# Decode attention beside a gated MLP: two-head tiles, product sums as identity matmuls, p.v with the values moving, a row maximum, one load queue

## The chip, the cores and the metric

The kernel runs on one core of one Trainium2 chip. The metric is the device time of a launch in microseconds, as the median of several runs; it was 710.52 us before the change (three runs, 710.52 to 710.72). A core has five engines with instruction queues of their own: TensorE (PE, matmuls; its weight loads are listed as PEld), VectorE (DVE), ScalarE (ACT), GpSimd (POOL) and SyncE (SP). Loads are issued from an engine's queue and moved by 16 DMA engines.

## What is computed

One decode step for four sequences: a layernorm of the input x, then attention over a cache of 4096 keys and values per head (32 heads of 128, each with its own keys and values), and beside it a small gated MLP on the same normalised input; both are added to x. Data are bf16.

```python
xn = layernorm(x)                                  # x: 4 x 1 x 640
q = (xn @ wq).reshape(4, 1, 32, 128).transpose(0, 2, 1, 3)
scores = einsum('bhqd,bhkd->bhqk', q, k_cache) * 128 ** -0.5   # k_cache: 4 x 32 x 4096 x 128
p = softmax(scores, axis=-1)
o = einsum('bhqk,bhkd->bhqd', p, v_cache)
A = o.transpose(0, 2, 1, 3).reshape(4, 1, 4096) @ wo           # wo: 4096 x 640

z = gelu(einsum('bsd,df->bsf', xn, w_in))          # w_in: 640 x 1728
z1, z2 = z[..., :864], layernorm(z[..., 864:])
g = einsum('ts,bsf->btf', w_sp, z2) + b_sp
B = einsum('bsf,fd->bsd', z1 * g, w_out)           # w_out: 864 x 640
return x + A + B
```

Keys and values are 2 x 134 MB; the weights together are some 14 MB. There is one query per head, so every key and value is used once.

## The kernel before

The main loop (L375) runs over 128 pairs of a head and a sequence, `idx = 4 * h + b`. For each, K and V of that head (4096 x 128, 1 MB each) lie in SBUF with 32 consecutive positions to each of the 128 lanes, so each lane holds one run of 8 KB. `issue_kv` (L113) loads them four iterations ahead, K from SP's queue (L118) and V from ScalarE's (L123), into pools of six buffers each.

Within an iteration:

- TensorE spreads the query row over all lanes by a matmul with a column of the identity (L391), and ScalarE copies it to bf16 (`qbc_sb`, L399).
- VectorE multiplies K by it (L402, 128 x 4096 elements), then sums the 128 products of each position: three halving additions from 128 to 16 elements (L411, 2048, 1024 and 512 elements a lane), and one reduction of the last 16 (L418). The scores are a 128 x 32 tile.
- ScalarE takes the exponential with the scale in it, and its sum over the lane goes into a column of `acc` (L425). No maximum is subtracted.
- TensorE forms p.v with V as the stationary operand: 32 matmuls, each of which loads 128 x 128 values and moves one column of p (L458). The result is a column of 128 values, copied to `o_all` by ScalarE (L466).

After four iterations (one head of all four sequences, L470) the lane sums are added by a matmul with ones (L473), inverted on VectorE (L481), spread over the lanes (L483), multiplied into the columns (L486), and the head's part of the output projection is added into a PSUM tile by two matmuls (L495, L502).

The queries are made in eight chunks of 512 columns (`compute_q_chunk`, five matmuls each, L196), and the pieces of wq and wo are loaded as the loop goes. The gated MLP is spread over iterations 16 to 28: its first projection (L217), the gelu, the layernorm, and its output projection (L348). At the end x, the MLP's part and the attention's part are added and stored (L516 to L519).

The order of instructions on each engine is found by the framework's scheduler. Engines are in-order queues: an instruction that waits holds up all that stands behind it on its engine.

Of the kernel before, what the change touches and what calls it, by code (L numbers as in the profile page):

```python
# [13 lines left out]
ALU = mybir.AluOpType  # L14

KV_BUFS = int(os.environ.get("PSGQA_KV_BUFS", "4"))
KV_SLACK = int(os.environ.get("PSGQA_KV_SLACK", "2"))
V_ENG = os.environ.get("PSGQA_V_ENG", "scalar")
RED_W = int(os.environ.get("PSGQA_RED_W", "16"))
O_COPY_ENG = os.environ.get("PSGQA_OCOPY", "scalar")  # L20
GMLP_AT = int(os.environ.get("PSGQA_GMLP_AT", "16"))
S_BUFS = int(os.environ.get("PSGQA_S_BUFS", "4"))
T_BUFS = int(os.environ.get("PSGQA_T_BUFS", "2"))
PV_ROW = int(os.environ.get("PSGQA_PV_ROW", "0"))
# [3 lines left out]
def kernel(  # L28
# [16 lines left out]

# [6 lines left out]
    NH = Bsz * H  # L52
    FHC = 108
    assert Fh % FHC == 0
    NFC = Fh // FHC
    NBLK = S // P
    scale_qk = float(Dh) ** -0.5
    eps = 1e-5
    assert Dh == P and HD == H * Dh
    N0 = 512  # L60
    NQC = HD // N0
    HPQ = N0 // Dh
    ITER_PER_CHUNK = HPQ * Bsz
    NZC = 2 * NFC
    NHALF = D // 2

    const = ctx.enter_context(tc.tile_pool(name="const", bufs=1))
    wts = ctx.enter_context(tc.tile_pool(name="wts", bufs=1))
    work = ctx.enter_context(tc.tile_pool(name="work", bufs=2))
    kpool = ctx.enter_context(tc.tile_pool(name="kpool", bufs=KV_BUFS + KV_SLACK))  # L70
    vpool = ctx.enter_context(tc.tile_pool(name="vpool", bufs=KV_BUFS + KV_SLACK))
    spool = ctx.enter_context(tc.tile_pool(name="spool", bufs=S_BUFS))
    tpool = ctx.enter_context(tc.tile_pool(name="tpool", bufs=T_BUFS))
    gpool = ctx.enter_context(tc.tile_pool(name="gpool", bufs=3))
    wqp = ctx.enter_context(tc.tile_pool(name="wqp", bufs=3))
    wop = ctx.enter_context(tc.tile_pool(name="wop", bufs=3))
    ps_misc = ctx.enter_context(tc.tile_pool(name="ps_misc", bufs=2, space=bass.MemoryType.PSUM))
    ps_out = ctx.enter_context(tc.tile_pool(name="ps_out", bufs=1, space=bass.MemoryType.PSUM))
    ps_q = ctx.enter_context(tc.tile_pool(name="ps_q", bufs=2, space=bass.MemoryType.PSUM))
    ps_o = ctx.enter_context(tc.tile_pool(name="ps_o", bufs=2, space=bass.MemoryType.PSUM))  # L80

    wsp_bf = const.tile([1, 1], BF16)
    nc.sync.dma_start(out=wsp_bf[:], in_=B_w_sp[0:1, 0:1])
    bsp_bf = const.tile([1, 1], BF16)
    nc.sync.dma_start(out=bsp_bf[:], in_=B_b_sp.rearrange("(a b) -> a b", a=1))
    x_bf = const.tile([Bsz, D], BF16)
    nc.sync.dma_start(out=x_bf[:], in_=A_x.flatten_outer_dims())

    wq_v = A_wq.rearrange("(c p) n -> p c n", p=P)
    wq_tiles = {}  # L90

    def issue_wq(j):
        if j < 0 or j >= NQC or j in wq_tiles:
            return
        wq_sb = wqp.tile([P, DC, N0], BF16)
        nc.sync.dma_start(out=wq_sb[:], in_=wq_v[:, :, j * N0 : (j + 1) * N0])
        wq_tiles[j] = wq_sb

    wo_v = A_wo.rearrange("(j hh p) n -> j p hh n", hh=HPQ, p=P)
    wo_tiles = {}  # L100

    def issue_wo(j):
        if j < 0 or j >= NQC or j in wo_tiles:
            return
        wo_sb = wop.tile([P, HPQ, D], BF16)
        nc.sync.dma_start(out=wo_sb[:], in_=wo_v[j])  # L106
        wo_tiles[j] = wo_sb

    issue_wq(0)

    kv_tiles = {}

    def issue_kv(i):  # L113
        if i >= NH or i in kv_tiles:
            return
        hh, bb = divmod(i, Bsz)
        k_nat = kpool.tile([P, NBLK, Dh], BF16)
        nc.sync.dma_start(  # L118
            out=k_nat[:], in_=A_k_cache[bb, hh].rearrange("(p c) d -> p c d", c=NBLK)
        )  # L120
        v_nat = vpool.tile([P, NBLK, Dh], BF16)
        veng = {"gpsimd": nc.gpsimd, "sync": nc.sync, "scalar": nc.scalar}[V_ENG]
        veng.dma_start(  # L123
            out=v_nat[:], in_=A_v_cache[bb, hh].rearrange("(p c) d -> p c d", c=NBLK)
        )
        kv_tiles[i] = (k_nat, v_nat)

    for i in range(KV_BUFS):
        issue_kv(i)
    issue_wo(0)  # L130
    issue_wq(1)
    issue_wo(1)

    w_in_sb = wts.tile([P, DC, F], BF16)
    nc.sync.dma_start(out=w_in_sb[:], in_=B_w_in.rearrange("(c p) n -> p c n", p=P))
    w_out_sb = wts.tile([FHC, NFC, D], BF16)
    nc.sync.dma_start(  # L137
        out=w_out_sb[:], in_=B_w_out.rearrange("(c p) n -> p c n", p=FHC)
    )

    ident = const.tile([P, P], BF16)
    make_identity(nc, ident[:])
    ones_col = const.tile([P, 1], FP32)
# [4 lines left out]
    nc.vector.memset(eps_tile[:], eps)  # L148

# [5 lines left out]
    for i in range(NSTAT):  # L155
# [5 lines left out]
        out=rstd[:],  # L161
        in_=mv[:, 1:2],
        func=ACT.Sqrt,
        bias=eps_tile[:Bsz],
        scale=1.0,
# [11 lines left out]
    xnT_ps = ps_misc.tile([P, DC, Bsz], BF16, tag="m")  # L177
    for c in range(DC):
        nc.tensor.transpose(
            out=xnT_ps[:, c, :],  # L180
            in_=xn_bf[:, c * P : (c + 1) * P],
            identity=ident[:Bsz, :Bsz],
        )
    xnT_sb = const.tile([P, DC, Bsz], BF16)
    nc.vector.tensor_copy(out=xnT_sb[:], in_=xnT_ps[:])

    q_rows = const.tile([Bsz, HD], BF16)
    q_done = set()

    def compute_q_chunk(j):  # L190
        if j in q_done or j >= NQC:
            return
        wq_sb = wq_tiles.pop(j)
        q_ps = ps_misc.tile([Bsz, N0], FP32, tag="m")
        for c in range(DC):
            nc.tensor.matmul(  # L196
                out=q_ps[:],
                lhsT=xnT_sb[:, c, :],
                rhs=wq_sb[:, c, :],
                start=(c == 0),  # L200
                stop=(c == DC - 1),
            )
        nc.vector.tensor_copy(out=q_rows[:, j * N0 : (j + 1) * N0], in_=q_ps[:])  # L203
        q_done.add(j)

    compute_q_chunk(0)

    res_sb = const.tile([Bsz, D], FP32)
    gm = {}

    def gmlp_stage_zT(k0, k1):
        if "zT_ps" not in gm:
            gm["zT_ps"] = ps_misc.tile([FHC, NZC, Bsz], FP32, tag="m", name="zT_ps")
        zT_ps = gm["zT_ps"]
        for k in range(k0, k1):
            for c in range(DC):
                nc.tensor.matmul(  # L217
                    out=zT_ps[:, k, :],
                    lhsT=w_in_sb[:, c, k * FHC : (k + 1) * FHC],
                    rhs=xnT_sb[:, c, :],  # L220
                    start=(c == 0),
                    stop=(c == DC - 1),
                )

    def gmlp_stage_gelu():
        zT_ps = gm["zT_ps"]
        zz = work.tile([FHC, NZC, Bsz], FP32)
        nc.vector.tensor_copy(out=zz[:], in_=zT_ps[:])
        gw = work.tile([FHC, NZC, Bsz], FP32)
        nc.vector.tensor_tensor(out=gw[:], in0=zz[:], in1=zz[:], op=ALU.mult)  # L230
        nc.vector.tensor_scalar(
            out=gw[:],
            in0=gw[:],
            scalar1=0.044715,
            scalar2=1.0,
            op0=ALU.mult,
            op1=ALU.add,
        )
        nc.vector.tensor_tensor(out=gw[:], in0=gw[:], in1=zz[:], op=ALU.mult)
        gt = work.tile([FHC, NZC, Bsz], FP32)  # L240
# [6 lines left out]
        gz = work.tile([FHC, NZC, Bsz], FP32)  # L247
        nc.vector.tensor_tensor(out=gz[:], in0=zz[:], in1=gt[:], op=ALU.mult)
        gm["gz"] = gz
        sq = work.tile([FHC, NFC, Bsz], FP32)  # L250
# [3 lines left out]
        gm["sq"] = sq  # L254

    def gmlp_stage_ln():
        gz = gm["gz"]
        sq = gm["sq"]
        wsp_t = work.tile([1, 1], FP32)
        nc.vector.tensor_copy(out=wsp_t[:], in_=wsp_bf[:])  # L260
        bsp_t = work.tile([1, 1], FP32)
        nc.vector.tensor_copy(out=bsp_t[:], in_=bsp_bf[:])
        s_ps = ps_misc.tile([1, 2 * Bsz], FP32, tag="m")
        for k in range(NFC):
            nc.tensor.matmul(
                out=s_ps[:, 0:Bsz],
                lhsT=ones_col[:FHC, :],
                rhs=gz[:, NFC + k, :],
                start=(k == 0),
                stop=(k == NFC - 1),  # L270
            )
        for k in range(NFC):
            nc.tensor.matmul(
                out=s_ps[:, Bsz : 2 * Bsz],
                lhsT=ones_col[:FHC, :],
                rhs=sq[:, k, :],
                start=(k == 0),
                stop=(k == NFC - 1),
            )
        st = work.tile([1, 5 * Bsz], FP32)  # L280
# [5 lines left out]
        inv_fh = 1.0 / float(Fh)  # L286
        nc.vector.tensor_scalar(
            out=mean_t, in0=s_ps[:, 0:Bsz], scalar1=inv_fh, scalar2=None, op0=ALU.mult
        )
        nc.vector.tensor_scalar(  # L290
            out=ex2_t,
            in0=s_ps[:, Bsz : 2 * Bsz],
            scalar1=inv_fh,
# [6 lines left out]
            out=rst_t, in_=var_t, func=ACT.Sqrt, bias=eps_tile[:1], scale=1.0  # L300
        )
        nc.vector.reciprocal(out=rst_t, in_=rst_t)
        ACrow = work.tile([1, 2 * Bsz], FP32)
        nc.vector.tensor_scalar(
            out=ACrow[:, 0:Bsz],
            in0=rst_t,
# [68 lines left out]
    for idx in range(NH):  # L375
# [11 lines left out]
        for fn in gmlp_schedule.get(idx, []):  # L387
            fn()
# [161 lines left out]
```

## Time and profile before

| | |
|---|---|
| median of three runs | 710.52 us |
| profiled execution, from first to last instruction | 707.1 us |
| read from HBM in it | 282.24 MB |
| VectorE busy | 644.0 us |
| TensorE matmuls busy | 230.7 us |
| ScalarE busy | 94.8 us |
| loads, 100 to 660 us | 418 GB/s |
| loads, 683 to 707 us | 25 GB/s |
| product L402, 128 x 4096 | 2282 ns |
| halving additions L411, 2048 / 1024 / 512 elements | 1215 / 681 / 413 ns |
| reduction L418, 512 elements to 32 | 671 ns |
| exponential L425 and its sum | 229 + 187 ns |
| matmul L495, 512 columns | 586 ns |
| f32 matmul L483, 128-column weights: weight load / matmul | 306 / 360 ns |

A page of a profile is the record of one execution. "Busy" is the time in which an engine carried out instructions. In a line of the groups, the name of the tile written stands left of the arrow and those read stand right of it; then come the shapes, the number of instructions, the busy time in us, the mean ns of one, and the idle time just before them with what ended it. An f32 matmul appears as two instructions. The 40 slices show shares of busy time in tenths along the span, and PEclk the clock that was granted to TensorE, in tenths of full speed.

### The profile page before, as it was taken

What the parts mean: (1) busy time and instruction counts of PE and PEld (TensorE: products, weight loads), DVE (VectorE), ACT (ScalarE), POOL (GpSimd) and SP (SyncE); (2) the same over time, 40 slices, a digit from 0 to 9 for tenths busy, and PEclk for the clock granted to TensorE, in tenths of its full rate; (3) what the DMA queues carried; (4) which work ended last, traced back from release to release, by engine and by line L of the source; (5) the groups of instructions that cost most, each with busy time, mean ns of one, the idle gap of its engine ahead of it and who ended that gap; (6) DMA issues with size and microseconds to landing.
All of it is one profiled execution on the core that took longest, in us unless ns stands there. A gap on an engine that the chain in (4) does not pass through costs nothing.

```text
span 707.1 us, 11278 instructions
## 1 busy us (share of the span) xinstructions
PE 230.7 (33%) x4591; PEld 171.6 (24%) x4591; DVE 644.0 (91%) x747; ACT 94.8 (13%) x519; POOL 0.7 (0%) x6
## 2 busy tenths in 40 slices
PE   1211243635343243322333342223433234332332
PEld 0110122523222222222222222222222222222221
DVE  1925999999999999999999989999999999999996
ACT  0200111111211111111011111111111111111110
POOL 0000000000000000000000000000000000000000
PEclk9999999999975555555555555555555555555555
DMA  8999999999999999999999999999999999999960
GB/s 348 403 359 411 419 419 406 417 416 420 412 421 419 416 420 412 419 417 419 419 413 421 416 420 421 420 413 416 421 420 421 420 419 421 419 421 420 419 273 1
DMA packets 47940, 282.99 MB, mean 400 GB/s; under 512 B 4392, under 2 KB 14480, under 8 KB 15120
## 3 DMA queue, kind: packets, MB, share of 16 engines
q1 hardware_dynamic: 29456, 148.04, 51.6%
q10 hardware_dynamic: 18432, 134.23, 45.9%
q8 instruction: 36, 0.59, 0.3%
q14 instruction: 16, 0.13, 0.0%
HBM read 282.24 MB, written 0.01 MB: 399 GB/s over the span
## 4 chain that ended last, share of the span: by engine, by line
DVE 64%; DMA 22%; PE 6%; issue 4%; SPq 3%; ACT 0%; DVEq 0%; ACTq 0%
DVE tmp L402 31%; DVE tmp L411 28%; DMA k_nat<-in_A_k_cache_dram 21%; DVE s_sb L418 3%; PE bc_ps L483 2%; PE q_ps L196 2%; SPq L118 2%; SPq L106 1%; DMA v_nat<-in_A_v_cache_dram 1%; PE g_ps L348 1%; DVE q_rows L203 1%; SPq L137 1%; PE out_ps L495 1%; DVE recip L481 0%; DVE o_norm L486 0%
## 5 line engine op out<-in xcount | busy, mean ns | idle before, releaser
L402 DVE TENSOR_TENSOR tmp<-k_nat,qbc_sb 128x4096 bf16<-128x4096 bf16 x128 | 292.0, 2282 | 24.0 <-DMA k_nat<-in_A_k_cache_dram 22.7
L411 DVE TENSOR_TENSOR tmp<-tmp 128x2048 bf16<-128x2048 bf16 (+2 forms) x384 | 282.4, 770 | 0.1
L458 PEld LDWEIGHTS <-v_nat 128*128 128x128 bf16 x4096 | 124.6, 104 | 423.3 <-issue 364.6
L458 PE MATMUL o_ps<-p_sb,v_nat 128*128 128x1 bf16 x4096 | 127.0, 165 | 225.9 <-ACT p_sb L425 203.9
L391 PE MATMUL qbc_ps<-q_rows,ident 4*128 4x128 bf16 x128 | 34.1, 269 | 170.9 <-ACT qbc_sb L399 170.2
L418 DVE TENSOR_REDUCE s_sb<-tmp 128x32 f32<-128x512 bf16 x128 | 85.7, 671 | 0.0
L425 ACT ACTIVATE p_sb<-s_sb 128x32 bf16<-128x32 f32 x128 | 29.4, 229 | 258.1 <-DVE s_sb L418 235.2
L399 ACT CAST qbc_sb<-qbc_ps 128x128 bf16<-128x128 f32 x128 | 32.8, 258 | 176.7 <-DVE tmp L402 107.7
L466 ACT COPY o_all<-o_ps 128x1 f32<-128x1 f32 x128 | 20.3, 159 | 165.0 <-PE o_ps L458 157.1
L483 PE MATMUL bc_ps<-recip,ones_row 1*128 1x4 f32 x64 | 18.7, 360 | 51.6 <-DVE recip L481 51.6
L483 PEld LDWEIGHTS bc_ps<-recip,ones_row 1*128 1x128 f32 x64 | 15.9, 307 | 55.2 <-DVE recip L481 55.2
L425 ACT ACTIVATION_READ_ACCUMULATOR p_sb<-s_sb 128x1 f32 x128 | 23.9, 187 | 0.2
L196 PE MATMUL q_ps<-wq_sb,xnT_sb 128*4 128x512 bf16 x40 | 19.8, 624 | 6.4 <-DMA wq_sb<-in_A_wq_dram 6.4
L495 PE MATMUL out_ps<-wo_sb,o_norm 128*4 128x512 bf16 x32 | 19.1, 598 | 8.4 <-DVE o_norm L486 8.4
L203 DVE CAST q_rows<-q_ps 4x512 bf16<-4x512 f32 x8 | 5.4, 678 | 16.9 <-PE q_ps L196 16.9
L486 DVE TENSOR_TENSOR o_norm<-o_all,bc_ps 128x4 bf16<-128x4 f32 x32 | 5.1, 158 | 8.0 <-PE bc_ps L483 7.9
L391 PEld LDWEIGHTS <-ident 4*128 4x128 bf16 x128 | 9.4, 105 | 8.3 <-issue 7.1
L502 PE MATMUL out_ps<-wo_sb,o_norm 128*4 128x128 bf16 x32 | 10.0, 312 | 0.0
L217 PE MATMUL zT_ps<-xnT_sb,w_in_sb 128*108 128x4 bf16 x80 | 7.8, 233 | 0.0
L217 PEld LDWEIGHTS <-w_in_sb 128*108 128x108 bf16 x80 | 7.6, 216 | 0.6 <-issue 0.5
L196 PEld LDWEIGHTS <-xnT_sb 128*4 128x4 bf16 x40 | 3.9, 110 | 13.7 <-issue 13.2
L481 DVE RECIPROCAL recip<-den_ps 1x4 f32<-1x4 f32 x32 | 5.3, 164 | 2.0 <-PE den_ps L473 2.0
(59 smaller groups left out, 40.5 us busy)
## 6 DMA issues: line engine op xcount, KB each, us to landing
v_nat<-in_A_v_cache_dram ACTq DMA_DIRECT2D x128, 1024.0 KB, 12.0
k_nat<-in_A_k_cache_dram SPq DMA_DIRECT2D x128, 1024.0 KB, 19.8
wq_sb<-in_A_wq_dram SPq DMA_DIRECT2D x8, 640.0 KB, 20.0
wo_sb<-in_A_wo_dram SPq DMA_DIRECT2D x8, 640.0 KB, 18.7
w_in_sb<-in_B_w_in_dram SPq DMA_DIRECT2D x1, 2160.0 KB
w_out_sb<-in_B_w_out_dram SPq DMA_DIRECT2D x1, 1080.0 KB
wsp_bf<-in_B_w_sp_dram SPq DMA_DIRECT2D x1, 0.0 KB
bsp_bf<-in_B_b_sp_dram SPq DMA_DIRECT2D x1, 0.0 KB
```

The costliest lines, as they stand in the source:

```text
L196: nc.tensor.matmul(out=q_ps[:], lhsT=xnT_sb[:, c, :], rhs=wq_sb[:, c, :], start=(c == 0), stop=(c == DC - 1),)
L217: nc.tensor.matmul(out=zT_ps[:, k, :], lhsT=w_in_sb[:, c, k * FHC : (k + 1) * FHC], rhs=xnT_sb[:, c, :], start=(c == 0), stop=(c == DC - 1),)
L391: nc.tensor.matmul(out=qbc_ps[:], lhsT=ident[:Bsz, b : b + 1].to_broadcast([Bsz, P]), rhs=q_rows[:, h * Dh : (h + 1) * Dh], start=True, st ...
L399: nc.scalar.copy(out=qbc_sb[:], in_=qbc_ps[:])
L402: nc.vector.tensor_tensor(out=tmp[:], in0=k_nat[:], in1=qbc_sb[:, None, :].to_broadcast([P, NBLK, Dh]), op=ALU.mult,)
L411: nc.vector.tensor_tensor(out=tmp[:, :, 0:h2], in0=tmp[:, :, 0:h2], in1=tmp[:, :, h2:w], op=ALU.add,)
L418: nc.vector.tensor_reduce(out=s_sb[:], in_=tmp[:, :, 0:w], axis=mybir.AxisListType.X, op=ALU.add,)
L425: nc.scalar.activation(out=p_sb[:], in_=s_sb[:], func=ACT.Exp, scale=scale_qk, accum_out=acc[:, col : col + 1],)
L458: nc.tensor.matmul(out=o_ps[:, :], lhsT=v_nat[:, c, :], rhs=p_sb[:, c : c + 1], start=(c == 0), stop=(c == NBLK - 1),)
L466: nc.scalar.copy(out=o_all[:, col : col + 1], in_=o_ps[:])
L483: nc.tensor.matmul(out=bc_ps[:], lhsT=ones_row[:, :], rhs=recip[:], start=True, stop=True)
L495: nc.tensor.matmul(out=out_ps[:, 0:N0], lhsT=lhsT, rhs=cur_wo[:, hh, 0:N0], start=first_proj, stop=last,)
```

## The change

The attention is written anew; the gated MLP's arithmetic stays.

- **Tiles.** A tile is now two heads of one sequence. The 2 x 4096 positions are laid over the lanes with 64 consecutive ones each, so lanes 0 to 63 hold the first head and 64 to 127 the second, and each lane has one run of 16 KB. There are 64 such tiles. K and V share one pool of seven 16 KB slots, and all loads are issued from SP's queue, K before V; at the end both last K tiles come before the last two V tiles, and the last V in four parts. All of wq is loaded first, into the same slots. The weights are laid out so that a lane's run is contiguous.
- **Queries.** All eight chunks are made before the loop, and copied by ScalarE.
- **Scores.** The products are formed on VectorE as before, in two halves of 32 positions. Their sums from 128 to 16 are made on TensorE: eight matmuls with the identity as weights, which add eight groups of 16 columns into one PSUM bank. VectorE reduces the last 16.
- **Maximum.** For each tile VectorE takes the maximum over a lane, TensorE turns the column of 128 into a row, VectorE takes the (negated) maximum of each half, and two f32 matmuls spread it, scaled, back over the lanes as the bias of the exponential.
- **p.v.** p is kept in a zeroed tile of 8 columns per position, one column for each of the two heads and four sequences. A matmul takes 4 positions (32 columns) as weights and moves 512 columns of V; 16 of them make a tile. They add into a 32 x 512 PSUM tile over four sequences, in which only blocks on the diagonal are wanted.
- **Groups.** After four tiles (two heads of all sequences) `group_a` to `group_d` copy that tile, add the lane sums, pick and add the diagonal blocks with f32 matmuls, normalise, turn, and project. They are spread over two iterations.
- **Sums at the end.** x and the MLP's part are added into the output's PSUM tile by matmuls.
- **Order.** On TensorE, VectorE and ScalarE the loop's order is the order in which it is written.

```diff
+KV_SLOTS = 7
+KV_AHEAD = 6
...
+    for c0, c1 in ((0, 2), (2, 4), (4, 5)):
+        t = kv.tile([P, 2, HD], BF16, tag="kv", name="wq")
+        nc.sync.dma_start(out=t[:, 0 : c1 - c0, :], in_=wq_v[:, c0:c1, :])
...
+    def load_k(i):
+        if i < NT:
+            k_tiles[i] = kv.tile([P, NC, Dh], BF16, tag="kv", name="k_nat")
+            nc.sync.dma_start(out=k_tiles[i][:], in_=kv_view(A_k_cache, i))
...
+    load_to(4)
+    nc.sync.dma_start(out=w_in_sb[:], in_=B_w_in.rearrange("(p c) n -> p c n", c=DC))
+    nc.sync.dma_start(out=w_out_sb[:], in_=B_w_out.rearrange("(p c) n -> p c n", c=NFC))
+    load_wo(0)
...
+    halves = const.tile([1, 2, P], FP32)
...
+    sel = const.tile([CG * NR, CG, NR], FP32)
...
+    def sums(i, half):
+        t = prods.pop((i, half))
+        s_ps = ps_s.tile([P, NH2, RW], FP32, name="s_ps")
+        for g in range(Dh // RW):
+            nc.tensor.matmul(
+                out=s_ps[:], lhsT=ident[:], rhs=t[:, :, g * RW : (g + 1) * RW],
...
+    def turn_max(i):
+        mT = ps_m.tile([1, P], FP32, tag="m", name="mT")
+        nc.tensor.transpose(out=mT[:], in_=maxes[i][:], identity=ident_f[:])
...
+    def spread_max(i):
+        nb_ps = ps_m.tile([P, 1], FP32, tag="m", name="nb_ps")
+        for hh in range(2):
+            nc.tensor.matmul(out=nb_ps[:], lhsT=halves[:, hh, :], rhs=maxes[i][:, hh : hh + 1],
...
+    def exps(i):
+        nc.scalar.copy(out=nb[:], in_=maxes.pop(i)[:])
+        for hh in range(2):
+            nc.scalar.activation(out=pm[ps, :, row], in_=s_sb[ps, :], func=ACT.Exp,
+                bias=nb[ps, :], scale=scale_qk, accum_out=a[ps, row : row + 1])
+
+    def weighted(i):
+        for g in range(n):
+            nc.tensor.matmul(
+                out=pvs[hp][:],
+                lhsT=pm[:, g * CG : (g + 1) * CG, :],
+                rhs=v_nat[:, g * CG : (g + 1) * CG, :],
...
+    def group_a(hp):
+        nc.scalar.copy(out=pv_sb[:], in_=pvs.pop(hp)[:])
+        nc.tensor.matmul(out=den[:], lhsT=acc[hp % NACC][:], rhs=ones_col[:], start=True, stop=True)
+        nc.vector.reciprocal(out=rden[:], in_=den[:])
+
+    def group_b(hp):
+        for j in range(CG):
+            nc.tensor.matmul(out=o_ps[:], lhsT=sel[:, j, :], rhs=pv_sb[:, j, :],
...
+        nc.vector.tensor_scalar(out=o_n[:], in0=o_ps[:], scalar1=rden[:, 0:1], scalar2=None, op0=ALU.mult)
...
+    with tc.manual_schedule(engines=ordered):
+        for i in range(NT + 3):
+            load_to(2 * i + KV_AHEAD)
+            if i % 8 == 1:
+                load_wo(i // 8 + 1)
+            at(i, products, 0)
+            at(i - 1, row_sums, 1)
+            at(i - 1, lane_max)
+            at(i, sums, 0)
+            at(i - 1, turn_max)
+            at(i + 2, stage_q)
+            group(i - 2, group_b)
+            at(i, products, 1)
+            at(i - 1, head_max)
+            at(i - 1, spread_max)
+            at(i - 1, exps)
+            at(i, sums, 1)
+            at(i, row_sums, 0)
+            group(i - 2, group_c)
+            at(i - 1, weighted)
+            group(i - 1, group_a)
+            group(i - 2, group_d)
+            if i in gmlp:
+                gmlp[i]()
```

`at(i, f)` calls f for tile i where it exists, `group(i, f)` calls f where i is the last tile of a group of four. `group_c` turns the normalised rows by eight small matmuls, `group_d` projects every second group by eight matmuls of 320 columns. `head_max` is the negated maximum of each half of the turned row, `lane_max` that of each lane.

## The prediction

> **What bounds the kernel now.** I read the busy table and the 40 slices first, then the chain of waits, then the costliest groups, then a table by stage.
>
> ```profile
> PE 230.7 (33%) x4591; PEld 171.6 (24%) x4591; DVE 644.0 (91%) x747; ACT 94.8 (13%) x519; POOL 0.7 (0%) x6
> ...
> PEclk9999999999975555555555555555555555555555
> DMA  8999999999999999999999999999999999999960
> GB/s 348 403 359 411 419 419 406 417 416 420 412 421 419 416 420 412 419 417 419 419 413 421 416 420 421 420 413 416 421 420 421 420 419 421 419 421 420 419 273 1
> ...
> DVE 64%; DMA 22%; PE 6%; issue 4%; SPq 3%; ACT 0%; DVEq 0%; ACTq 0%
> ...
> L402 DVE TENSOR_TENSOR tmp<-k_nat,qbc_sb 128x4096 bf16<-128x4096 bf16 x128 | 292.0, 2282 | 24.0 <-DMA k_nat<-in_A_k_cache_dram 22.7
> L411 DVE TENSOR_TENSOR tmp<-tmp 128x2048 bf16<-128x2048 bf16 (+2 forms) x384 | 282.4, 770 | 0.1
> ```
>
> Two things are full at once. VectorE is busy 91%, and the loads run at about 420 GB/s until some 683 us, after which VectorE works off what is buffered until the end at 707 us. A head (2.10 MB) takes 2.10/0.42 = 5.0 us to load; VectorE needs 644/128 = 5.03 us for it. So a change gains only if it lightens both, and removing VectorE work alone stops at the loads: 282.24 MB / 0.42 = 672 us plus start and tail. TensorE is 33% busy, and with matmuls one column wide; that cheap engine is where the change puts the work. What TensorE costs per column is therefore the question:
>
> ```profile
> 15.96 2.29 PE L196 MATMUL q_ps<-wq_sb,xnT_sb 128*4 128x512 bf16 x5 [6.42 <-DMA wq_sb<-in_A_wq_dram]
> ```
> ```profile
> L348 PE MATMUL g_ps<-w_out_sb,yT x16: 339/474/475, 193.8 to 198.3; 108*4 108x320 bf16 x16
> ```
> ```profile
> 196.00:197.00 1.00, 1.00 (x6) 0.45 (x5) 0.32 (x1) 0.00 (x0) 0.00 (x0) 1.00 1.01 418
> ...
> 201.00:202.00 1.00, 0.00 (x0) 0.00 (x0) 1.00 (x2) 0.22 (x1) 0.00 (x0) 0.89 1.03 426
> 202.00:203.00 1.00, 0.51 (x11) 0.35 (x11) 1.00 (x2) 0.37 (x3) 0.00 (x0) 0.50 1.02 426
> ```
> ```profile
> 256.40 0.59 PE L483 MATMUL bc_ps<-recip,ones_row 1*128 1x4 f32 x2 [1.09 <-DVE recip L481]
> 256.92 1.87 PE L196 MATMUL q_ps<-wq_sb,xnT_sb 128*4 128x512 bf16 x4
> ```
>
> The first line is the timeline: five 512-column matmuls in 2.29 us; less the last one's 0.585 us (the shortest of L196) that is 0.426 us apart. The second is a line's durations, shortest/median/longest: the last 320-column matmuls, at 198.3 us, took 339 ns where the median took 474, 0.42 ns per column less. So 512 columns cost 0.426 us at half clock and 0.426 - 512 x 0.42/1000 = 0.21 us at full. The windows (the clock is the third value from the end) show when: after TensorE had been solid from 193.3 us, the fast ones come, and by 202 us, with hardly a column streamed in between, the clock is back at 0.50. (The 1.00 before 198 us can't be the true clock, for the 0.426 us spacing at 16 us falls under it; I take it as nothing recorded yet.) The same happens after the solid stretch at 256.4 us and one at 338 us. Full speed is therefore granted after about 3.4 us of solid columns.
>
> **The change, part by part.** All durations are of the profiled execution, span 707.1 us, last transfer included; the median of runs, 710.52 us, lies 3.4 us above it. I add 3 at the end.
>
> VectorE: the 384 halving adds go (282 us). Products stay 128 x 2.28, reductions 128 x 0.67 (L418, same 512 elements, now from PSUM; L228 from PSUM and L230 from SBUF both take 215 ns, so I price PSUM at nothing). Added: 64 lane maxima and 64 head maxima at about 0.2 to 0.25 (64 elements: 215 ns). Sum 292 + 86 + 28 = 406 us, 6.3 of the 10.0 us in which a two-head tile loads. VectorE is no longer the bound.
>
> Loads: the same bytes. One queue for two costs nothing while SP only issues (0.33 us per issue). In the queue table the ACT queue's 8 KB runs take 45.9% x 16 x 707.1 = 5193 us; the SP queue carries as much K in the same time and 13.8 MB of short weight runs in the remaining 645 us, where the 8 KB rate would need 534: longer weight runs gain at most 111/16 = 7 us. For 16 KB against 8 KB no row exists; between 0 and the gain per byte already seen (some 2%, 13 us) I take 0. The whole wq now precedes the first K, so q is ready near 30 us where the first product started at 19.6; that is hidden, since tile 2's K is the 19.7th MB (wq 5.2, two tiles 8.4, the rest of the weights 4.0, K 2.1), lands at 2 + 47 = 49 us and holds the pipeline there anyway. Loads alone would end the kernel at 2 + 672 + 12 (tail) = 686 us.
>
> TensorE, per two-head tile: 16 sums and 16 weighted matmuls of 512 columns replace 64 of one column: 32 x 0.21 = 6.7 us full, 13.7 half. The maximum adds turn_max (f32, 128 columns: between one pass at full clock, 0.05, and four at half, 0.43; I take 0.2), and spread_max, two f32 matmuls with 128-column weights, for which L483 is the row: 0.50 us of weight load for each pair of instructions, so 1.0 us; if that load too follows the clock, 0.5. stage_q 0.1. TensorE waits for head_max, which stands on VectorE behind the second product: 0.3. Behind spread_max are queued the second sums and weighted. Ordinary tile, full clock: 6.7 + 0.2 + 0.1 + 0.3 + 1.0 = 8.3 us.
>
> Every fourth tile a group ends. group_b: four f32 matmuls of 128 columns, 0.2 to 1.7, by the same passes 0.85; group_c 8 x 0.06; den 0.19 (L473 pair); half of group_d's 8 x 320 columns, 0.53. Together 2.1. Two new waits matter more. rden stands on VectorE ahead of the next first product but waits for den, which TensorE does after weighted: then recip, hand-over and a whole product, 0.16 + 0.1 + 2.2 = 2.5 us in which TensorE has nothing. In the following tile o_n, on VectorE ahead of the second product, waits for group_b: another 0.2 + 0.1 + 2.2 = 2.5. Four tiles: 4 x 8.3 + 2.1 + 5.0 = 40.3 us, 10.1 per tile, against 40.0 of loads. With both unknowns low, 4 x 7.65 + 1.4 + 5.0 = 37.0; high, 42.
>
> So at full clock TensorE and the loads are level. TensorE: tile 2 starts at 49 + 2 = 51; 62 tiles x 10.1 = 626; the gated MLP on the same queue about 15 (90 pairs of L217's kind, 8.1 us per 80; 18 x 0.13; a VectorE chain that it waits for, 3.5); tail 12 (last weighted 3.4, softmax chain 2, group steps 4, output 2.5). 704 us in the span, of which nothing is spare.
>
> The clock decides. Solid stretches (second sums, weighted, next first sums: 6.8 us) are long enough to win full clock; the gaps are 1.6 us in ordinary tiles and 2.5 to 3 at the two group waits. A loss costs one to two 3.4 us stretches at half speed, 2.5 us of lost columns. No loss: 704. One per four tiles: 16 x 2.5 = 40, **744**. One per tile: 160, 864. No row shows a gap of 2 to 3 us between dense stretches; the nearest is the 201 us one, over 2 us almost empty, and it lost the clock. I take one loss per group.
>
> The Trainium skill, "TensorE: Matmul & The Clock Gate", "Part 1: The HAM clock gate", states that full speed holds until a whole window of about 3.4 us is idle; by that no gap here loses it and the sum would be 704. The same page, "A second HAM failure mode: psum-queue depth-cycling", speaks against the change: matmul groups that cycle PSUM banks with short idle spells make the clock swing, which would be the 744 to 864 side.
>
> **Rivals.** (1) The forecast: TensorE bound, clock lost about once per group, 744 + 3 = 747; own range 722 to 790; 0.42. (2) Clock kept, TensorE and loads level: 704 + 3 = 707, from 690 to 724 by the unknowns; for it, the 6.8 us stretches; 0.24. (3) The other side, faster: the loads set the end at 686 + 3 = 689. One mechanism: TensorE's four-tile period under 40.0 us, which needs the clock kept and weight loads and f32 passes at their low prices (37.0). For it: 9.9 in the DMA row shows nothing else would hold it; against it: L483's price; 0.16. (4) The clock falls at every tile's gap: 790 to 870; for it, a record of 0.50 for nearly all of this execution; 0.18.
>
> **Numbers.** About 0.2% (1.4 us) is what can be told from no change. Case 3 is faster, case 2 about half, with 0.03 within 0.2%; the rest slower: 0.28, 0.03, 0.69. The range leaves out the far end of (4) and a gain on the 16 KB runs: 684 to 835.
>
> **What would show it.** Right: DMA slices falling to 8 or 9 tenths with K loads waiting for freed slots, VectorE near 60% with idle time ended by TensorE at rden and o_n, the chain mostly PE, a clock row between 0.8 and 1. Wrong: 0.42 us spacing of sums throughout (4), or DMA at 420 GB/s to the end with PE waiting for K (3). A granted clock of 1.00 with a time above 730 would mean that a matmul with 128-column weights costs more than its columns.

## The result: 10% slower, TensorE bound, and the profile after

The changed kernel takes 782.02 us (median of four runs, 778.97 to 782.49) against 710.52 us before: the ratio is 1.1006, with a 95% interval from 1.0984 to 1.1028. 747 us was forecast, in a range of 684 to 835: the slowdown is 71.5 us where 36.5 were forecast. The profiled execution has a span of 780.4 us. Its busy table, slices, chain and costliest groups:

```profile
PE 651.0 (83%) x3041; PEld 294.6 (38%) x3041; DVE 406.9 (52%) x455; ACT 123.9 (16%) x432; POOL 2.6 (0%) x12
...
PEclk9978868878779898978999897989999897979998
DMA  8999998749679599996999799996999799998910
GB/s 361 425 370 427 427 427 348 307 196 403 296 269 406 205 433 423 426 428 249 430 427 426 317 423 429 428 412 249 427 425 426 325 428 427 427 427 355 416 44 1
...
PE 76%; DVE 12%; DMA 9%; issue 1%; ACT 1%; SPq 1%
...
L403 PE MATMUL s_ps<-prod,ident 128*128 128x512 bf16 x1024 | 292.6, 437 | 52.6 <-DVE prod L390 52.6
L390 DVE TENSOR_TENSOR prod<-k_nat,qbc 128x4096 bf16<-128x4096 bf16 x128 | 291.0, 2274 | 42.2 <-DMA k_nat<-in_A_k_cache_dram 24.8
L477 PE MATMUL pv<-v_nat,pm 128*32 128x512 bf16 x1024 | 243.0, 392 | 2.4 <-ACT pm L461 2.4
L403 PEld LDWEIGHTS <-ident 128*128 128x128 bf16 x1024 | 101.7, 108 | 189.3 <-issue 117.7
```

VectorE fell from 644 to 407 us and from 91 to 52%, as it was meant to. TensorE has taken its place: 83% busy, 76% of the chain. The loads, which ran flat at 420 GB/s before, run at 427 where they run, and drop to 200 to 350 in one slice of some four. The drops follow from TensorE: SP's queue waits for the p.v matmuls that still read a slot, and six times the load of the next piece of `wo` waits for the output projection and holds up the K and V loads behind it (total us, number of waits, longest):

```profile
SPq L107 <- PE pv L477: 303.4, 37, 13.2
...
SPq L134 <- PE out_ps L542: 114.0, 6, 20.4
```

The drops don't set the time: products wait for K only four times, 24.8 us in all, 16.8 of it once at the start. The clock row is no longer 5 but swings between 6 and 9 (0.885 in the mean).

One group of four tiles, 43.8 us, shows the mechanism. From the timeline (start, duration, engine and line, in square brackets the idle time before it and what ended it), from the tile with the den wait to the tile with group_b:

```profile
417.25 1.90 PE L403 MATMUL s_ps<-prod,ident 128*128 128x512 bf16 x8
...
422.00 3.63 PE L477 MATMUL pv<-v_nat,pm 128*32 128x512 bf16 x16
...
425.70 0.15 DVE L496 RECIPROCAL rden<-den 8x1 f32<-8x1 f32 x1 [5.53 <-PE den L492]
425.79 2.26 DVE L390 TENSOR_TENSOR prod<-k_nat,qbc 128x4096 bf16<-128x4096 bf16 x1
...
428.10 1.89 PE L403 MATMUL s_ps<-prod,ident 128*128 128x512 bf16 x8 [2.45 <-DVE prod L390]
...
431.27 0.34 DVE L511 TENSOR_SCALAR o_n<-o_ps,rden 8x128 bf16<-8x128 f32 x1 [2.37 <-PE o_ps L503]
431.54 2.27 DVE L390 TENSOR_TENSOR prod<-k_nat,qbc 128x4096 bf16<-128x4096 bf16 x1
...
434.16 0.98 PE L444 MATMUL nb_ps<-nm,halves 1*128 1x1 f32 x4 [2.92 <-DVE nm L432]
...
435.07 3.60 PE L403 MATMUL s_ps<-prod,ident 128*128 128x512 bf16 x8
```

VectorE has been idle for 5.53 us when den comes; only then may it start the next product, and TensorE stands 2.45 us. In the next tile o_n waits for group_b and holds the second product: TensorE stands 2.92 us. After that gap the same eight sums take 3.60 us instead of 1.90: the clock has gone. The windows around it (PE, PEld, DVE, ACT and POOL busy, then clock, DMA share, GB/s) say so too; in the last one the loads stand still, for none is issued between 425.65 and 444.57 us, when `wo` goes and K, V and K follow at once:

```profile
428.00:434.00 6.00, 3.13 (x19) 1.47 (x18) 3.60 (x7) 0.27 (x1) 0.00 (x0) 1.00 1.01 431
434.00:437.00 3.00, 2.84 (x9) 1.66 (x10) 2.80 (x3) 1.32 (x5) 0.00 (x0) 0.51 0.99 421
437.00:441.00 4.00, 4.00 (x18) 1.33 (x17) 2.26 (x3) 0.16 (x1) 0.00 (x0) 0.51 0.90 381
441.00:445.00 4.00, 4.00 (x23) 1.86 (x22) 0.84 (x1) 0.00 (x0) 0.00 (x0) 1.00 0.06 25
```

Behind the second wait the clock is at half in every group. The first one kept it here, but not everywhere: in the eleven groups that begin between 252 and 688 us the eight sums behind it take 1.89 us in six and 2.86 to 3.40 us in five, at the same 2.45 us of idle time. The next group is one of the five:

```profile
471.92 3.40 PE L403 MATMUL s_ps<-prod,ident 128*128 128x512 bf16 x8 [2.45 <-DVE prod L390]
```

### The profile page after: what moved, and what is told of

It is laid out like the page before. It is cut to its first block, busy times and chain, and to the rows that moved or that the text cites. A ratio compares the mean times of both kernels' runs of the same rounds, so it can differ in the third digit from the quotient of the medians.

```text
span 780.4 us, 7465 instructions
## 1 busy us (share of the span) xinstructions
PE 651.0 (83%) x3041; PEld 294.6 (38%) x3041; DVE 406.9 (52%) x455; ACT 123.9 (16%) x432; POOL 2.6 (0%) x12
## 4 chain that ended last, share of the span: by engine, by line
PE 76%; DVE 12%; DMA 9%; issue 1%; ACT 1%; SPq 1%
PE s_ps L403 34%; PE pv L477 29%; DVE prod L390 9%; PE nb_ps L444 5%; DMA w_in_sb<-in_B_w_in_dram 5%; DMA k_nat<-in_A_k_cache_dram 4%; PE o_ps L503 2%; PE zT L244 2%; DVE nm L432 2%; PE out_ps L542 1%; PE mT L427 1%; DVE o_n L511 1%; PE qbc_ps L375 1%; PE oT_ps L523 0%; PE out_ps L348 0%
## 5 line engine op out<-in xcount | busy, mean ns | idle before, releaser
L403 PE MATMUL s_ps<-prod,ident 128*128 128x512 bf16 x1024 | 292.6, 437 | 52.6 <-DVE prod L390 52.6
L390 DVE TENSOR_TENSOR prod<-k_nat,qbc 128x4096 bf16<-128x4096 bf16 x128 | 291.0, 2274 | 42.2 <-DMA k_nat<-in_A_k_cache_dram 24.8
L477 PE MATMUL pv<-v_nat,pm 128*32 128x512 bf16 x1024 | 243.0, 392 | 2.4 <-ACT pm L461 2.4
L403 PEld LDWEIGHTS <-ident 128*128 128x128 bf16 x1024 | 101.7, 108 | 189.3 <-issue 117.7
L477 PEld LDWEIGHTS <-pm 128*32 128x32 bf16 x1024 | 96.6, 99 | 139.4 <-ACT pm L461 20.4
L413 DVE TENSOR_REDUCE s_sb<-s_ps 128x32 f32<-128x512 f32 x128 | 86.2, 673 | 33.1 <-PE s_ps L403 33.1
L444 PE MATMUL nb_ps<-nm,halves 1*128 1x1 f32 x256 | 45.0, 276 | 57.1 <-DVE nm L432 55.2
L461 ACT ACTIVATE pm<-s_sb,nb 64x64 bf16<-64x64 f32 x128 | 74.0, 578 | 3.3 <-ACT nb L456 0.2
L444 PEld LDWEIGHTS nb_ps<-nm,halves 1*128 1x128 f32 x256 | 40.2, 221 | 68.8 <-issue 47.3
L461 ACT ACTIVATION_READ_ACCUMULATOR pm<-s_sb,nb 64x1 f32 x128 | 41.9, 327 | 0.0
```

The source lines that it names most:

```text
L390: nc.vector.tensor_tensor(out=t[:], in0=k_tiles[i][:, cs, :], in1=qbcs[i][:, None, :].to_broadcast([P, NH2, Dh]), op=ALU.mult,)
L403: nc.tensor.matmul(out=s_ps[:], lhsT=ident[:], rhs=t[:, :, g * RW : (g + 1) * RW], start=(g == 0), stop=(g == Dh // RW - 1),)
L413: nc.vector.tensor_reduce(out=scores[i][:, half * NH2 : (half + 1) * NH2], in_=sums_ps.pop((i, half))[:], axis=AX.X, op=ALU.add,)
L444: nc.tensor.matmul(out=nb_ps[:], lhsT=halves[:, hh, :], rhs=maxes[i][:, hh : hh + 1], start=(hh == 0), stop=(hh == 1),)
L461: nc.scalar.activation(out=pm[ps, :, row], in_=s_sb[ps, :], func=ACT.Exp, bias=nb[ps, :], scale=scale_qk, accum_out=a[ps, row : row + 1],)
L477: nc.tensor.matmul(out=pvs[hp][:], lhsT=pm[:, g * CG : (g + 1) * CG, :], rhs=v_nat[:, g * CG : (g + 1) * CG, :], start=(b == 0 and g == 0) ...
```

## Experiments

The theory: the order of work on TensorE sets the time; 32 dense matmuls and the maximum make a tile 8.3 us at full clock, two waits of a group add 5 us and cost the clock as well. Rivals: the loads with their seven slots and one queue are the limit; the row maximum alone is the difference; the clock falls for a reason that has nothing to do with the gaps. Medians below stand beside 782.0 for the changed kernel; ratios are to the kernel before, run on the same chip (709.9 to 710.3 us in these series).

**e1_late_groups: the two waits taken away.** `rden` moves behind the head maximum, `group_b` with `o_n` behind the second sums, `group_c` behind `weighted`.

```diff
             at(i + 2, stage_q)
-            group(i - 2, group_b)
             at(i, products, 1)
             at(i - 1, head_max)
+            group(i - 2, group_r)
...
             at(i, row_sums, 0)
-            group(i - 2, group_c)
+            group(i - 2, group_b)
             at(i - 1, weighted)
             group(i - 1, group_a)
+            group(i - 2, group_c)
             group(i - 2, group_d)
```

> The reciprocal of den and the scaling of o_n move behind work that VectorE has anyway (the reciprocal behind the head maximum, group_b and o_n behind the second sums), so that no product waits for them. Theory (TensorE's order sets the time, and the two gaps of 2.5 to 2.9 us also cost the clock): a group of four tiles goes from 43.8 us to about 4 x 8.3 + 2.6 = 35.8 on TensorE, below the 39.3 us that its loads take at 427 GB/s; the loads then set the end, 675 to 700 us, clock over 0.95. Rival A (the loads, with seven slots and one queue, set the time now): no change, 775 to 785. Rival B (the clock falls at shorter gaps too, once TensorE has time to spare): 715 to 760.

Measured: 712.37 us, ratio 1.0027 (1.0004 to 1.0049), clock 0.953. A gain of 70 us, so rival A is out, but 12 us more than the theory's 700 at most. Rival B's range is missed by 3 us on the other side; the clock does fall at two shorter gaps (2.15 us at 338 us, 2.07 us at 579 us), but there TensorE waits for a K that is still being loaded. The slices show where the 12 us are:

```profile
PEclk9987987998889999999999999999999989999999
DMA  8999999969969899999999999999999999999980
GB/s 351 429 367 426 428 426 426 426 250 428 404 259 392 351 435 424 428 426 424 429 426 426 425 428 426 425 428 426 426 424 429 426 428 423 427 429 427 426 355 1
```

From the 15th slice on (248 us) the loads are full and the clock at 9 but for one slice; between 140 and 248 us they drop to 250 and 259. That is where the MLP stands (tiles 5 to 13), and what the loads lose there can't be made up.

**e2_no_max: the row maximum left out.** The lane maximum, turn, head maximum, spread and bias are not computed.

```diff
-            at(i - 1, lane_max)
...
-            at(i - 1, turn_max)
...
-            at(i - 1, head_max)
-            at(i - 1, spread_max)
...
-                bias=nb[ps, :],
```

> The row maximum is left out (no lane maximum, turn, head maximum, spread and bias), as in the kernel before the change. Theory: an ordinary tile loses 1.3 us of TensorE (turn 0.2, spread 0.5, wait 0.3 to 0.6); a group takes 4 x 7.0 + 2.6 + 5.0 + 3.4 = 39.0 us, level with the loads: 690 to 720. Rival A (loads): no change, 775 to 785. A rival in which the maximum is the whole difference to the kernel before (the group waits count for nothing): 705 to 712 and a clock of 1.

Measured: 709.39 us, ratio 0.9982 (0.9966 to 0.9999), clock 0.903. The maximum costs 73 us in the changed kernel, in the theory's range. By time alone the rival "the maximum is everything" would also fit; its clock of 1 doesn't, and e1, which keeps the maximum and gains 70 us, rules it out. Groups after 225 us take 39 to 41 us (the last one 35), which is what the loads take, and the clock is lost again in each: the maximum is as large a piece as the group waits, and either one hides behind the loads once the other is gone.

**e3_fill: spare matmuls in the two gaps.**

```diff
+    def fill(n):
+        f_ps = ps_m.tile([P, N0], FP32, tag="m", name="f_ps")
+        for c in range(n):
+            nc.tensor.matmul(out=f_ps[:], lhsT=ident[:], rhs=w_in_sb[:, c % DC, 0:N0], ...)
...
             group(i - 2, group_b)
+            group(i - 2, lambda hp: fill(10))
...
             group(i - 1, group_a)
+            group(i - 1, lambda hp: fill(10))
```

> Ten spare matmuls of 512 columns, whose result nobody reads, stand in each of the two gaps of a group (behind den and behind group_b); they add work and take no wait away. Theory (the gap costs its own time and, besides, 3.4 us of lost columns by the clock): from the third group on the clock stays at 1.00 and a group takes about 40.4 instead of 43.8 us; 725 to 750 in all. Rival (only the gap itself costs, the clock falls for another reason): 780 or more, with the same 0.88 clock.

Measured: 731.75 us, ratio 1.0314 (1.0268 to 1.0361): 50 us faster by adding work. The timeline shows the gaps filled and the sums behind them at full speed, the window from 200 to 600 us a clock of 1.00 (second fence; the third is the same window of the changed kernel):

```profile
440.57 2.33 PE L491 MATMUL f_ps<-w_in_sb,ident 128*128 128x512 bf16 x10
443.09 1.89 PE L403 MATMUL s_ps<-prod,ident 128*128 128x512 bf16 x8 [0.19 <-DVE prod L390]
...
446.15 2.33 PE L491 MATMUL f_ps<-w_in_sb,ident 128*128 128x512 bf16 x10
449.05 0.60 PE L444 MATMUL nb_ps<-nm,halves 1*128 1x1 f32 x4 [0.57 <-DVE nm L432]
449.59 1.90 PE L403 MATMUL s_ps<-prod,ident 128*128 128x512 bf16 x8
```
```profile
200.00:600.00 400.00, 385.49 (x1977) 174.40 (x1976) 244.77 (x256) 71.55 (x260) 0.00 (x0) 1.00 0.97 408
```
```profile
200.00:600.00 400.00, 342.74 (x1658) 153.40 (x1657) 226.02 (x249) 66.83 (x238) 0.00 (x0) 0.90 0.90 378
```

The waits themselves are all still there; a group from 240 us on takes 39.6 to 40.7 us (the last one 39.2), where the prediction's sum for full clock was 40.3. So the gaps do cost the clock, and holding it through them is worth 50 us.

**e4_slots6: one slot fewer.**

```diff
-KV_SLOTS = 7
-KV_AHEAD = 6
+KV_SLOTS = 6
+KV_AHEAD = 5
```

> Six slots for K and V instead of seven, and loads issued one tile-half less ahead. Theory (TensorE bound, loads wait for slots and not the other way round): 780 to 795. Rival A (slots and the one queue set the time): one slot is 5 us of lead less, 830 us or more.

Measured: 783.57 us, ratio 1.1042 (1.0997 to 1.1088), the same as the changed kernel. So the seven slots don't set the time; the dips in the loads follow from what they wait for on TensorE.

**e5_thin: the MLP spread.** The first projection goes in 18 pieces over tiles 6 to 23, each copied from PSUM by ScalarE; gelu and layernorm are cut at the hand-overs between engines, one piece a tile, and the output projection at tiles 30 and 31.

```diff
-    for i in range(6):
-        gmlp[5 + i] = lambda k0=3 * i: gmlp_z(k0, k0 + 3)
-    gmlp[11] = gmlp_gelu
-    gmlp[12] = gmlp_ln
-    gmlp[13] = gmlp_out
+    for i in range(NZC):
+        gmlp[6 + i] = lambda k=i: gmlp_z(k)
+    steps = (gmlp_gelu, gmlp_gelu_b, gmlp_ln, gmlp_ln_b, gmlp_ln_c, gmlp_ln_d)
+    for i, fn in enumerate(steps):
+        gmlp[6 + NZC + i] = fn
+    gmlp[30] = lambda: gmlp_out(0)
+    gmlp[31] = lambda: gmlp_out(1)
```

> The changed kernel with the MLP alone laid out otherwise: its first projection in 18 pieces of five matmuls over 18 tiles (6 pieces of 15 over 6 tiles before), and the gelu and the layernorm cut where one engine waits for another, one piece a tile. Theory: the 2.7 us stretches of four-column matmuls cost their own time and the clock; the three groups from 87 to 252 us took 59.5, 53.9 and 52.1 us, against 43.8 later; they come to some 46 to 48: 755 to 770. Rival (the MLP's work costs the same wherever it stands): 778 to 784.

Measured: 771.34 us, ratio 1.0855 (1.0828 to 1.0883): 11 us better, just outside the 755 to 770 expected. The three groups came down to 46.1, 46.4 and 46.8 us as foreseen, but the spread MLP now burdens the next four groups too (48.4, 46.9, 49.7, 45.5); I had left those out.

**e6_late_thin: both together.**

> Both: no product behind den and group_b, and the MLP spread. Theory: TensorE's group is 36 us plus about 1 us of MLP, always below the 39.3 us of loads, so nothing of the load time is lost after the start: 282.24 MB at 427 GB/s is 661 us, with 3 us at the start, some 5 of slot waits before 50 us, and a tail of 12 to 14: 680 to 692. Rival (seven slots hold the loads back even when TensorE keeps up): 700 to 710, as with the group steps moved alone.

Measured: 686.41 us, ratio 0.9665 (0.9642 to 0.9689), clock 0.979. This version beats both kernels with all of the computation kept, row maximum included. Its slices and the window from 200 to 600 us:

```profile
PEclk9986999999999999999999999999899999999999
DMA  8999999999999999999999999999999999999970
GB/s 349 430 366 430 433 429 428 433 426 432 432 430 430 430 429 430 431 426 432 432 432 430 428 432 428 432 429 430 432 430 430 427 434 431 428 430 429 433 318 2
```
```profile
200.00:600.00 400.00, 357.24 (x1880) 168.11 (x1879) 251.84 (x279) 75.64 (x275) 0.00 (x0) 0.99 1.01 430
```

The loads are flat at 430 GB/s from 51 to 650 us, and nothing is lost after the start. 70 and 11 us apart make 96 together: with the waits alone removed the loads still fell behind between 140 and 248 us, and with the MLP alone spread they still fell behind in group after group, down to 117 GB/s in one slice.

**e7_late_thin_8k and e8_late_thin_vact: run length and queue.** On top of e6, each tile is loaded in two transfers of 8 KB runs, or V is issued from ScalarE's queue.

```diff
-            nc.sync.dma_start(out=k_tiles[i][:], in_=kv_view(A_k_cache, i))
+            for j in range(2):
+                cs = slice(j * NH2, (j + 1) * NH2)
+                nc.sync.dma_start(out=k_tiles[i][:, cs, :], in_=kv_view(A_k_cache, i)[:, cs, :])
...
-                load_v(i, 4 if i == NT - 1 else 1)
+                load_v(i, 4 if i == NT - 1 else 2)
```
```diff
-                nc.sync.dma_start(
+                nc.scalar.dma_start(
                     out=v_tiles[i][:, j * n : (j + 1) * n, :],
```

> As the one before, but each K and V tile is loaded by two transfers of 8 KB runs. If the longer runs are what lifts the rate from 418 to 427 GB/s: 418 here, 2% or 13 to 15 us longer. If it is the single queue: 427 here too and the same time within 3 us.

> As e6_late_thin, but V is issued from ScalarE's queue, as in the kernel before the change. If the single queue lifts the rate: 418 GB/s here and 10 to 15 us longer; if the 16 KB runs do: 427 and the same within 3 us, unless an issue that waits for a slot on ScalarE holds up an exponential, which would show as a wait of TensorE for the exponential and 695 or more.

Measured: 690.40 us (0.9708, 0.9682 to 0.9734) and 692.05 us (0.9734, 0.9711 to 0.9758). The windows from 200 to 600 us, first with 8 KB runs, then with V on ScalarE's queue:

```profile
200.00:600.00 400.00, 356.38 (x1868) 167.00 (x1866) 249.99 (x277) 73.78 (x268) 0.00 (x0) 0.99 1.01 426
```
```profile
200.00:600.00 400.00, 367.49 (x1892) 170.88 (x1891) 254.38 (x281) 76.33 (x277) 0.00 (x0) 0.96 1.01 430
```

Run length: 426 against 430, 1% and 4 us, in the direction expected and a third of its 13 to 15 us; the number of transfers doubled with it, and the two weren't separated. Queue: no effect on the rate, but 5.6 us longer all the same. The waits for the exponentials are as in e6 (21.8 and 22.6 us in all, at the weight loads of p.v); the difference stands at the end. The first product of the last tile waits for its K until 663.05 us, where it begins at 657.47 in e6, 5.6 us earlier. That fits the order of the loads: on one queue the last two K tiles come ahead of the last two V tiles, on two queues nothing holds those V tiles back. An earlier lag (the third tile's first product begins at 64.7 us instead of 54.4) is caught up by then, for at 645.7 us VectorE has again waited 3.6 us for K.

**e9_late_thin_nomax: the maximum left out of e6.**

> As e6_late_thin, with the row maximum left out again (no lane maximum, turn, head maximum, spread and bias). Theory: with the group steps and the MLP out of the way the loads set the end, and the maximum's 1.3 us a tile lies in TensorE's spare time; it costs only its part of the tail (turn, head maximum, spread of the last tile, some 1.5 us): 683 to 687. Rival (the maximum still costs through TensorE or the clock): 680 or less, or, if the emptier tiles lose the clock, 690 or more.

Measured: 681.04 us, ratio 0.9585 (0.9556 to 0.9614). That is 2 us below the theory's range and 1 us above the rival's. The maximum, worth 73 us in the changed kernel, is worth 5.4 us here. In the middle it is hidden, as expected: both load 430 GB/s from 200 to 600 us. The 1.5 us I gave it in the tail were too few. With it TensorE ends the last sums at 667.7 us, without it at 664.5; behind them the turn and the spread of the last tile with the idle times after the head maximum (0.37 us) and the exponential (1.45 us) take 2.7 us more, so the last weighted ends at 677.4 against 671.4.

## Why the prediction was right, and where its sizes were off

The direction, the bound and the mechanism held: TensorE took VectorE's place, an ordinary tile takes 8.30 us at full clock (408.95 to 417.25 in the timeline; 8.3 forecast), and the two named waits leave TensorE idle 2.45 and 2.92 us (2.5 each forecast) and cost the clock. Experiments e1 and e3 show the waits and the clock as causes; e4 takes the slots out as a cause, and e6, at 430 GB/s from one queue, the queue. But the slowdown is nearly twice the forecast, and the wide range did its part. The span was forecast at 744 and came to 780.4. By terms:

- *MLP on the queue, forecast 15 us, measured 34.* The three groups from 87 to 252 us took 59.5, 53.9 and 52.1 us, 165.5 against 3 x 43.7 later. This is the largest term that was mis-sized, 19 us, and for two reasons. The instructions themselves take longer: 90 pairs of weight load and matmul come in six stretches of 2.74 us, 16.4 us, where the row L217 gave 9.1. A weight load of 96 columns takes 267 ns in the median, one of 108 columns took 217 before; the columns now lie nine elements apart in `w_in_sb` and lay side by side before, but no run shows that this is the reason. And such a stretch of 15 four-column matmuls can cost the clock, which the sum left out: behind five of the six it is lost, and it is 0.78 in the mean between 85 and 225 us. Here the sums start at full clock and end at half:

```profile
133.97 2.74 PE L244 MATMUL zT<-xnT,w_in_sb 128*96 128x4 bf16 x15
136.57 3.08 PE L403 MATMUL s_ps<-prod,ident 128*128 128x512 bf16 x8
```

- *The clock, forecast one loss of 2.5 us a group, measured 3.4 us in 1.5 losses.* In the eleven groups between 252 and 732 us the spread, the sums and the weighted behind the second wait take 1.6 to 3.1 us longer than at full clock, 2.6 in the mean. That is the one loss, rightly sized. The losses behind the first wait, in five of the eleven, add 0.8 in the mean. So a group is 43.7 instead of 42.8: 14 us over the kernel. That there would be about one loss a group was a choice between cases, with one row of the kernel before, the almost empty 2 us at 201 us, to go by.
- *Start of tile 2, forecast 51 us, measured 56.6.* K of tile 2 landed at 54.2 us instead of 49. About 2 us of it are the load of `w_out`, by an estimate: its 1.1 MB go at some 225 GB/s instead of 427. From 42 to 46 us the packets have the 11,520 bytes of a lane's run of `w_out`, and the loads run at 220 to 230 GB/s with the DMA engines busy, as the last two values of the window show; why these packets are slow isn't shown.

```profile
42.00:44.00 2.00, 1.97 (x10) 0.78 (x8) 0.00 (x0) 0.00 (x0) 0.00 (x0) 1.00 1.01 230
```

- The three make 39 us, the miss is 36; the rest are small ones with the other sign.

The 8.3 us of a tile are right in sum only, and that is luck. The spread takes 0.60 us at full clock and 0.98 at half, and its f32 weight loads 0.52 and 0.93, so the weight load does follow the clock and the low end of its bounds was the right one. The 32 matmuls of 512 columns take 7.1 us from start to start instead of 6.7, and the query's spread 0.24 instead of 0.1. Taking L483 at half clock as the price at full was the slip, and it cancelled.

The rivals. "The loads set the end" needed the low prices and the clock kept; the first came true in part, the second didn't, and 430 GB/s makes the loads cheaper than the 420 that I used. It is what e6 became, at 686 against the 689 worked out for it, in part by luck: at 430 GB/s the loads alone take 656 us and not 672. "Clock kept, level" is what e3 shows, where spare matmuls keep the clock: 40.2 us a group. The rule of the Trainium skill's "TensorE: Matmul & The Clock Gate", "Part 1: The HAM clock gate", that a whole idle window is needed to lose full speed, differs from these traces: the 2.92 us gap, with 1 us of small f32 matmuls ahead of it, lost it in group after group, the 2.45 us gap in five of eleven, in e6 even one of 1.98 us, and the measurement decides. That page's second failure mode, small idle spells between groups of matmuls that make the clock swing, is closer to what happened.

The single queue was rightly priced at nothing, and the longer runs nearly so: e8 and e7 give 0% and 1%. The rise from 418 to 430 GB/s is 3%, and no run here explains the other 2%.

## What to carry to other kernels

When work moves from a full engine to an idle one, price it at the clock that it will get, and look in the new order for every instruction on the relieved engine that waits for the loaded one and stands ahead of what feeds it: here a reciprocal of eight numbers held up 2.2 us of product. Moving such small steps behind work that is there anyway, and spreading work that streams few columns, turned 10% slower into 3.4% faster with the same arithmetic. A fix that shows less than its worth may still be right: where loads are the floor, each stretch in which they fall behind has to go before the floor is reached.

## What the runs showed of the hardware that was not expected

Adding 4.3 us of spare matmuls to a group (20 x 0.213) made it 3.5 us shorter. Whether an idle spell of TensorE costs full clock isn't decided by its length alone. Behind 512-column matmuls, spells of up to 1.9 us kept it in e1, e6, e7 and e9; between 2.0 and 3.1 us both happen. Two of e9's, behind the same 16 weighted matmuls:

```profile
395.44 3.35 PE L418 MATMUL s_ps<-prod,ident 128*128 128x512 bf16 x8 [3.05 <-DVE prod L405]
474.78 1.89 PE L418 MATMUL s_ps<-prod,ident 128*128 128x512 bf16 x8 [3.09 <-DVE prod L405]
```

The first lost the clock, the second, slightly longer, kept it; what decides is not shown by any run here. The loads reach 430 GB/s with 16 KB runs and 426 with 8 KB runs; why the kernel before stayed at 418 with 8 KB runs is not settled, though its weights came in shorter ones.
